# A linear-attention and expert kernel on one core: the Gram products at the end of an iteration, half of the spread transfers, a prologue in written-out order

## The chip, the cores and the metric

The kernel runs on one core of a Trainium2 chip. The metric is device time in microseconds (us) of one execution, as the median of several runs. Engines: PE is TensorE, DVE is VectorE, ACT is ScalarE, POOL is GpSimd, SP is SyncE, which here only issues DMAs. ACT issues DMAs too.

## The reference, cut to what matters

```python
k_n = k / (norm(k) + 1e-6)                     # (4, 8, 768, 48): 32 heads, 768 tokens, width 48
for t in range(S):                             # deltanet: one 48x48 state per head
    y[:, :, t] = q[:, :, t] @ state
    v_old = k_n[:, :, t] @ state
    state += beta[t] * outer(k_n[:, :, t], v[:, :, t] - v_old)
x = y.transpose(0, 2, 1, 3).reshape(3072, 384)
logits = x @ w_gate                            # 8 experts
expert = argmax(logits); gate_w = softmax(logits)[expert]
for e in range(8):                             # of each expert's tokens the 80 with the largest gate_w
    out[tok] = gate_w[tok] * (relu(x[tok] @ w1[e]) @ w2[e])
```

## The kernel before, in words

The 768 tokens of a head are cut into 12 chunks of 64, and a chunk of all 32 heads is worked on at once. Inside a chunk the recurrence becomes the inverse of a 64x64 triangular matrix per head. That inverse is built from 16x16 diagonal blocks: `solve` inverts them, and products with `XB` and `YB`, block-diagonal tiles that hold the small inverses, put the large inverse `Y` together.

What is done for chunk c, with the engine that does it:

- `load_k`, `load_q`, `load_v` fetch raw k (`kr`), q (`qn`) and v (`vin`); SP issues them.
- `squares` (ACT) and `newton` (DVE, some 15 small instructions) make 1/norm; `scale_k` (POOL) makes `kn`; `beta_mask` (POOL) makes a mask times beta.
- `trans`: PE transposes `kn` and `qn`, ACT copies the result to `KQ`.
- `gram`: PE multiplies `KQ` with itself; DVE turns each half into `B1` and `PT`; ACT issues two DMAs of `B1` to DRAM (`a_blocks`). `fetch` reads the 16x16 blocks back (`NT`); ACT issues it.
- `solve`: 30 POOL instructions on `NT` leave `XY`, the inverses and their transposes.
- `spread`: SP writes `XY` to DRAM (`inv_blocks`, named i_dram in the code) and then reads it back into `XB` with 8 small DMAs. `spread_t` reads it into `YB` with 4 DMAs of SP and 4 of ACT.
- `merge_p2` (needs `XB`), `merge_x4` (needs `YB`), `merge_y4`, `merge_p5`, `merge_y5`: PE products with an eviction each, on DVE (`P2`, half of `P5`) or ACT.
- The chain over the chunks: `chain_ks` (PE, then R on DVE), `chain_tr` (PE, then `UB` on DVE), `chain_qs`, `chain_ku` (updates the state in PSUM, ACT copies it to `SB`), `chain_pu` (ACT copies the output x, SP writes it to `x_rows`).
- `out_t` and `logits`: x is transposed, multiplied with the gate's weights, and DVE copies the result to `lg`. One part `zero` of the output is cleared per iteration by an SP DMA.

The order is written out by hand: each engine executes its instructions in the order of the program text. One loop over j from -4 to 11 is a software pipeline: iteration j does the chain of chunk j, the merges of j+1, the spread of j+2, `gram`, `fetch` and `solve` of j+3, and `scale_k` and `trans` of j+4. The first four iterations (j<0) are the prologue, with most calls empty.

Small DVE work that nobody waits for at once stands in a list of generators, `fillers`: `newton`; `gate` (some 24 instructions on the logits of a batch of three chunks); and `gate_top` (10 pairs of a maximum and a replacement, which keep the largest gate values). `fill(n)` puts the next n steps in at its place: 20 after `chain_pu`, 10 ahead of `merge_p2`, 4 after `logits`. Every third iteration `gate_pe` transposes gate values on PE, after `fill(100)` has emptied the list.

PSUM products share three buffers in rotation (`mtile`), so a product waits for the eviction of the third one before it. The DMAs of SP and ACT share eight completion semaphores in turn: a DMA also waits until the previous DMA on its semaphore has landed, whichever engine issued that one.

After the loop come the tail of the gate, the selection of 80 tokens per expert on DVE and PE, gathers on POOL, and the eight experts' products (`hp`, `yp`).

Of the kernel before, what the change touches and what calls it, by code (L numbers as in the profile page):

```python
# [24 lines left out]
def kernel(  # L25
# [22 lines left out]
    nc = tc.nc  # L48
# [105 lines left out]
    with ExitStack() as actx:  # L154
# [93 lines left out]
        def newton(bs):  # L248
# [4 lines left out]
            for n, c in enumerate(bs):  # L253
                nc.vector.tensor_reduce(ss[:, n * NB : (n + 1) * NB], ssq.pop(c), axis=AX, op=Alu.add)
                yield 1
            seed = sml.tile([128, 2 * NB], U32, name="seed")[:, :G]
            nc.vector.tensor_scalar(seed, ss.bitcast(U32), -0.5, 1597463007.0, op0=Alu.mult, op1=Alu.add)
            yield 1
            r = seed.bitcast(F32)
            for _ in range(3):  # L260
                t = sml.tile([128, 2 * NB], F32, name="nt")[:, :G]
                nc.vector.scalar_tensor_tensor(out=t, in0=ss, scalar=-0.5, in1=r, op0=Alu.mult, op1=Alu.mult)
                yield 1
                nc.vector.tensor_tensor(out=t, in0=t, in1=r, op=Alu.mult)
                yield 1
                rn = sml.tile([128, 2 * NB], F32, name="rn")[:, :G]
                nc.vector.scalar_tensor_tensor(out=rn, in0=t, scalar=1.5, in1=r, op0=Alu.add, op1=Alu.mult)
                yield 1
# [3 lines left out]
            yield 1  # L272
            nc.vector.tensor_scalar_add(n, n, 1e-6)
            yield 1
# [4 lines left out]
            yield 1  # L279

        def scale_k(c):
            if ok(c):
                nc.gpsimd.tensor_tensor(out=kn[c % NKB][:, :, 0:D], in0=kr.pop(c),
                                        in1=inv.pop(c).unsqueeze(2).to_broadcast([128, NB, D]), op=Alu.mult)
# [47 lines left out]
        def solve(c):  # L332
# [3 lines left out]
            XY = Xss[c] = sml.tile([128, 2, 16, 16], F32, name="XY")  # L336
            X = XY[:, 0]
            nc.gpsimd.tensor_tensor(out=X, in0=NT.rearrange("p s t -> p t s"), in1=eye16, op=Alu.add)  # L338
            for t in range(14, 0, -1):
                sh = [128, 15 - t, t]  # L340
                tmp = sml.tile([128, 64], F32, name="tmp")
                tv = tmp[:, : (15 - t) * t].rearrange("p (c s) -> p c s", s=t)
                nc.gpsimd.tensor_tensor(out=tv, in0=X[:, t + 1 :, t : t + 1].to_broadcast(sh),  # L343
                                        in1=NT[:, 0:t, t].unsqueeze(1).to_broadcast(sh), op=Alu.mult)
                nc.gpsimd.tensor_tensor(out=X[:, t + 1 :, 0:t], in0=X[:, t + 1 :, 0:t], in1=tv, op=Alu.add)  # L345
            nc.gpsimd.tensor_copy(XY[:, 1], X.rearrange("p t s -> p s t"))

        def spread(c):
# [4 lines left out]
            for e in range(2):  # L353
                for i in range(4):
# [3 lines left out]
        def spread_t(c, q):  # L358
# [156 lines left out]
        def gate(b):  # L515
# [4 lines left out]
            yield 1  # L520
            sh = sml.tile(full, F32, name="sh")
            nc.vector.tensor_tensor(out=sh, in0=l, in1=mx.unsqueeze(2).to_broadcast(full), op=Alu.subtract)
            yield 1
# [3 lines left out]
            yield 1  # L527
            fm = sml.tile([128, NT], F32, name="fm")
            nc.vector.tensor_reduce(fm, first, axis=AX, op=Alu.max)
            yield 1  # L530
            oh = sml.tile(full, F32, name="oh")
            nc.vector.tensor_tensor(out=oh, in0=first, in1=fm.unsqueeze(2).to_broadcast(full), op=Alu.is_equal)
            yield 1
            nc.vector.tensor_scalar_max(sh, sh, -87.0)
            yield 1
            n = sml.tile(full, F32, name="n")
            nc.vector.tensor_scalar(n, sh, LOG2E, None, op0=Alu.mult)
            yield 1
            nc.vector.tensor_scalar_add(n, n, ROUND)
            yield 1  # L540
            nc.vector.tensor_scalar_add(n, n, -ROUND)
            yield 1
            r = sml.tile(full, F32, name="r")
            nc.vector.scalar_tensor_tensor(out=r, in0=n, scalar=-LN2_HI, in1=sh, op0=Alu.mult, op1=Alu.add)
            yield 1
            nc.vector.scalar_tensor_tensor(out=r, in0=n, scalar=-LN2_LO, in1=r, op0=Alu.mult, op1=Alu.add)
            yield 1
            ex = sml.tile(full, F32, name="ex")
            nc.vector.tensor_scalar(ex, r, 1.0 / 5040.0, None, op0=Alu.mult)
            yield 1  # L550
            for f in (720.0, 120.0, 24.0, 6.0, 2.0, 1.0):
                nc.vector.scalar_tensor_tensor(out=ex, in0=ex, scalar=1.0 / f, in1=r, op0=Alu.add, op1=Alu.mult)
                yield 1
            nc.vector.tensor_scalar_add(ex, ex, 1.0)
            yield 1
            two = sml.tile(full, I32, name="two")
            nc.vector.tensor_scalar(two, n, 127.0, 8388608.0, op0=Alu.add, op1=Alu.mult)
            yield 1
            nc.vector.tensor_tensor(out=ex, in0=ex, in1=two.bitcast(F32), op=Alu.mult)
            yield 1  # L560
            gw = sml.tile([128, NT], F32, name="gw")
            nc.vector.tensor_reduce(gw, ex, axis=AX, op=Alu.add)
            yield 1
            nc.vector.tensor_scalar_add(gw, gw, 1e-9)
            yield 1
            nc.vector.reciprocal(gw, gw)
            yield 1
            og = ohg[:, b * NT : (b + 1) * NT, :]
            nc.vector.tensor_tensor(out=og, in0=oh, in1=gw.unsqueeze(2).to_broadcast(full), op=Alu.mult)
            yield 1  # L570
# [22 lines left out]
        def gate_top(b):  # L593
            cd, nx = cand[b % 2], cand[(b + 1) % 2]
            for t in range(TR):
                m8 = nx[:, t * 8 : t * 8 + 8]
                nc.vector.max(m8, cd)
                nc.vector.match_replace(cd, in_to_replace=m8, in_values=cd, imm_value=0.0)
                yield 1
# [6 lines left out]
        load_k(0)  # L606
# [15 lines left out]
        for c in squares([0]):  # L622
            for _ in newton([0]):
                pass
        nc.vector.tensor_copy(beta_t.rearrange("r c g -> r (c g)"), bps[:, 0, : NB * NC])
        S_ps = ps_s.tile([128, 2, 512], F32, name="S_ps")
        nc.vector.memset(S_ps, 0.0)
        nc.vector.memset(zero, 0.0)
        nc.vector.tensor_copy(P5.rearrange("r p g w -> r (p g) w"), eye.unsqueeze(1).to_broadcast([128, NB, 64]))

        for j in range(-4, NC):
            spread(j + 2)
            chain_ks(j)
# [18 lines left out]
            fill(20)  # L652
# [15 lines left out]
            if j >= GC and j % GC == 0:  # L668
# [3 lines left out]
            if j >= 0 and j % GC == GC - 1:  # L672
                fill(100)
# [168 lines left out]
```

## Time and the profile before

| | us |
|---|---|
| median of 3 runs | 514.31 (513.81 to 514.63) |
| the profiled execution, its own time | 510.11 |
| its span, first to last instruction | 508.1 |
| PE busy, all of the span | 354.1 |
| POOL busy | 190.6 |
| DVE busy | 213.2 |
| ACT busy | 117.5 |

`UB` is written once per chunk, by `chain_tr`; its first DVE instruction marks the iterations. In the profiled execution it starts at 89.88, 114.08, 139.97, 168.24, 193.79, 220.38, 244.22, 272.57, 293.39, 315.65, 336.47 and 351.88 us for the chunks 0 to 11. So the prologue lasts 89.88 us, the eleven intervals 262.0 us and what follows 156.2 us.

### The profile page before, as it was taken

The page shows a single profiled execution, that of the slowest core. Times are in us where ns is not written, and L with a number is a line of the kernel's source. Part 1 is how long each engine was busy: PE and PEld are TensorE (multiplying, and loading weights), DVE is VectorE, ACT ScalarE, POOL GpSimd, SP SyncE. Part 2 cuts the span into 40 slices and gives each one's busy share as a digit, 9 for nine tenths or more (in the row PEclk, how much of TensorE's full clock was granted, in tenths as well). Part 3 has the DMA queues.
Part 4 walks back from the last instruction along what each step waited for, and adds up shares of the span by engine and source line. Part 5 has one row for each costly group of instructions (what it writes and reads, how often), then busy time and mean ns, then how long its engine had stood idle before and what let it go on. Part 6 is the DMA issues. An engine that isn't in the chain of part 4 may idle for free. (4 is left out here: it accounts for less than half of the span.)

```text
span 508.1 us, 16641 instructions
## 1 busy us (share of the span) xinstructions
PE 354.1 (70%) x7227; PEld 311.8 (61%) x7239; DVE 213.2 (42%) x545; ACT 117.5 (23%) x207; POOL 190.6 (38%) x476
## 2 busy tenths in 40 slices
PE   2632574969695979697958996876100269999996
PEld 2632463959595968596847886876100167777773
DVE  4823202632353555833474923637659600010100
ACT  2120141606151434133321450422100000010000
POOL 8727576636272563618380725100200140000010
PEclk9965687979788899889979998989655557999999
DMA  9362857484819293746473454412739965980000
GB/s 163 66 113 66 121 108 149 75 178 84 176 30 204 37 186 70 165 83 131 95 157 65 107 100 114 83 38 65 234 107 409 411 220 161 316 294 15 10 17 14
DMA packets 198728, 66.48 MB, mean 131 GB/s; under 512 B 180704, under 2 KB 191968, under 8 KB 198656
## 3 DMA queue, kind: packets, MB, share of 16 engines
q1 hardware_dynamic: 134656, 54.69, 42.2%
q10 hardware_dynamic: 63232, 8.77, 10.5%
q0 software_dynamic: 768, 1.97, 1.3%
q8 instruction: 57, 0.93, 0.8%
q14 instruction: 15, 0.12, 0.1%
HBM read 45.53 MB, written 19.86 MB: 129 GB/s over the span
## 5 line engine op out<-in xcount | busy, mean ns | idle before, releaser
L343 POOL TENSOR_TENSOR tmp<-XY,NT 128x14 f32<-128x14 f32 (+6 forms) x168 | 48.2, 287 | 13.2
L338 POOL TENSOR_TENSOR XY<-NT,eye 128x256 f32<-128x256 f32 x12 | 10.2, 851 | 110.0 <-DMA NT<-a_blocks 110.0
L345 POOL TENSOR_TENSOR XY<-XY,tmp 128x14 f32<-128x14 f32 (+6 forms) x168 | 45.8, 273 | 13.2
L802 PEld LDWEIGHTS hp<-xTe,w 128*128 128x128 f32 x384 | 49.0, 210 | 2.1 <-issue 1.2
L207 PE MATMUL pm<-P,YB 64*64 64x32 f32 x768 | 22.7, 279 | 37.7 <-DMA YB<-inv_blocks 35.8
L802 PE MATMUL hp<-xTe,w 128*128 128x80 f32 x384 | 48.8, 292 | 0.0
L453 DVE TENSOR_TENSOR UB<-pm,beta_t 64x768 f32<-64x768 f32 x24 | 22.9, 955 | 60.2 <-PE pm L207 59.9
L207 PEld LDWEIGHTS pm<-P,YB 64*64 64x64 f32 x768 | 21.8, 206 | 39.5 <-issue 39.5
L810 PE MATMUL yp<-w,hT 128*80 128x384 f32 x128 | 44.0, 498 | 0.0
L814 POOL DMA_INDIRECT out_dram<-y,idx_s x8 | 7.4, 923 | 83.8 <-DVE y L813 83.8
L207 PE MATMUL pm<-KQ 48*64 48x128 f32 x768 | 29.2, 311 | 12.7 <-ACT KQ L301 7.1
L805 ACT ACTIVATE hT<-hp 128x320 f32<-128x320 f32 x16 | 7.0, 437 | 133.7 <-PE hp L802 133.7
L380 DVE TENSOR_TENSOR P<-pm,mask 128x512 f32<-128x512 f32 x24 | 15.5, 686 | 49.4 <-PE pm L207 49.4
L207 PE MATMUL pm<-SB,KQ 128*64 128x96 f32 x704 | 35.0, 254 | 1.2 <-DVE lg L511 1.2
L390 ACT COPY X<-pm 128x512 f32<-128x512 f32 x12 | 7.0, 586 | 122.4 <-PE pm L207 72.6
L207 PEld LDWEIGHTS pm<-KQ 48*64 48x64 f32 x768 | 25.8, 157 | 14.8 <-ACT KQ L301 7.8
L301 ACT COPY KQ<-pm 128x512 f32<-128x512 f32 x48 | 24.9, 613 | 34.8 <-PE pm L298 24.3
L207 PEld LDWEIGHTS pm<-SB,KQ 128*64 128x64 f32 x704 | 31.2, 141 | 2.2 <-PE pm L590 1.5
L810 PEld LDWEIGHTS yp<-w,hT 128*80 128x80 f32 x128 | 19.1, 155 | 20.2 <-issue 20.2
L207 PE MATMUL pm<-XB,B 128*64 128x128 f32 x384 | 25.3, 288 | 6.2 <-DMA YB<-inv_blocks 3.9
L207 PEld LDWEIGHTS pm<-XB,B 128*64 128x64 f32 x384 | 22.3, 144 | 9.6 <-issue 5.2
L813 DVE TENSOR_SCALAR y<-yp,gw_t 80x384 f32<-80x384 f32 x8 | 4.9, 613 | 54.7 <-PE yp L810 54.7
(163 smaller groups left out, 663.8 us busy)
## 6 DMA issues: line engine op xcount, KB each, us to landing
w<-in_moe_w_dram SPq DMA_DIRECT2D x16, 1536.0 KB, 7.3
a_blocks<-B ACTq DMA_DIRECT2D x24, 256.0 KB, 4.6
vin<-in_v_dram SPq DMA_DIRECT2D x26, 192.0 KB, 4.8
kr<-in_k_dram SPq DMA_DIRECT2D x24, 192.0 KB, 3.9
qn<-in_q_dram SPq DMA_DIRECT2D x24, 192.0 KB, 4.6
x_rows<-x SPq DMA_DIRECT2D x24, 192.0 KB, 2.7
out_dram<-zero SPq DMA_DIRECT2D x12, 384.0 KB, 2.6
inv_blocks<-XY SPq DMA_DIRECT2D x12, 256.0 KB, 2.9
```

Of the source, the lines that this page charges most:

```text
L207: nc.tensor.matmul(out, lhsT=lhsT, rhs=rhs, start=not acc, stop=not acc, skip_group_check=True)
L301: nc.scalar.copy(KQs[c][:, 4 * h : 4 * h + 4, n, :], pt[:, h].rearrange("r (g w) -> r g w", w=128))
L338: nc.gpsimd.tensor_tensor(out=X, in0=NT.rearrange("p s t -> p t s"), in1=eye16, op=Alu.add)
L343: nc.gpsimd.tensor_tensor(out=tv, in0=X[:, t + 1 :, t : t + 1].to_broadcast(sh), in1=NT[:, 0:t, t].unsqueeze(1).to_broadcast(sh), op=Alu.mult)
L345: nc.gpsimd.tensor_tensor(out=X[:, t + 1 :, 0:t], in0=X[:, t + 1 :, 0:t], in1=tv, op=Alu.add)
L380: nc.vector.tensor_tensor(out=P2[:, p].rearrange("r g e w -> r (g e) w"), in0=ps[:, p].rearrange("r (g w) -> r g w", w=64), in1=mask.unsqu ...
L390: nc.scalar.copy(X4s[c], ps[:, :, :256].rearrange("r b (g w) -> r b g w", w=32))
L453: nc.vector.tensor_tensor(out=UB[hs(e), :, e].rearrange("r (g c) d -> r c g d", c=2), in0=ps[hs(e), :, : 8 * D].rearrange("r c (g d) -> r ...
L802: nc.tensor.matmul(hp[:, (f - f0) * cap : (f - f0 + 1) * cap], lhsT=w1_t[:, c, f * 128 : (f + 1) * 128], rhs=xTs[e][:, c, :], start=(c == ...
L805: nc.scalar.activation(hT[:, f0:f1, :], hp[:, : (f1 - f0) * cap].rearrange("p (f t) -> p f t", t=cap), Act.Relu)
L810: nc.tensor.matmul(yp[:cap, :DM], lhsT=hT[:, f, :], rhs=w2_t[:, f, :], start=(f == 0), stop=(f == FK - 1))
L814: nc.gpsimd.indirect_dma_start(out=out[:, :], out_offset=bass.IndirectOffsetOnAxis(ap=idx_s[:, e : e + 1], axis=0), in_=y[:, :], element_o ...
```

## The change

`gram(j+4)` stands at the end of iteration j, between `out_t` and `logits`, where `gram(j+3)` stood near the start. `fetch(j+3)` and `solve(j+3)` follow `merge_p5`; `scale_k` and `beta_mask` of j+4 stand at the top; `merge_p2(j+2)` stands ahead of `out_t`. `spread` issues only the blocks that the later product with `mask` keeps (4 DMAs into `XB`, not 8). `spread_t` issues all 8 into `YB` on SP, right after `merge_y4`, and so ahead of the loads. `fill` takes an estimate in us (0.5 and 7.0 in an iteration), and each filler step names its own estimate. `gate_pe` moves one iteration later (j = 4, 7, 10). The prologue is written out; `solve(0)` and `solve(1)` run on DVE there.

```diff
-        def fill(n):
-            while n > 0 and fillers:
-                if next(fillers[0], None) is None:
+        def fill(us):
+            while us > 0 and fillers:
+                n = next(fillers[0], None)
+                if n is None:
                     fillers.pop(0)
                 else:
-                    n -= 1
+                    us -= n
...
-        def solve(c):
+        def solve(c, eng=nc.gpsimd):
...
             for e in range(2):
-                for i in range(4):
+                for i in (0, 2):
                     r = 64 * e + 16 * i
                     nc.sync.dma_start(XB[r : r + 16, :, e, 16 * i : 16 * i + 16], src[e, i, 0])
...
-            for h in range(2):
-                for i in range(4):
+            for i in range(4):
+                for h in range(2):
                     r = 64 * h + 16 * i
-                    if h == q:
-                        eng = (nc.sync, nc.scalar)[q]
-                        eng.dma_start(YB[r : r + 16, :, h, 16 * i : 16 * i + 16], src[h, i, 1])
+                    eng = nc.scalar if c == 0 and h else nc.sync
+                    eng.dma_start(YB[r : r + 16, :, h, 16 * i : 16 * i + 16], src[h, i, 1])
...
+        warm = sml.tile([128, 1], F32, name="warm", bufs=1)
+        nc.scalar.activation(warm, ident[:, 0:1], Act.Square)
...
+        trans(2, 1, qn[2 % NQB])
+        load_q(3)
+        fetch(0)
+        gram(2)
+        for t in (XB, YB, SB, UB):
+            nc.gpsimd.memset(t, 0.0)
+        solve(0, nc.vector)
+        spread(0)
+        spread_t(0)
+        fetch(1)
+        norms([3])
+        scale_k(3)
+        beta_mask(3)
+        load_k(6)
+        trans(3, 0, kn[3])
+        trans(3, 1, qn[3 % NQB])
+        load_q(4)
+        solve(1, nc.vector)
+        fetch(2)
+        solve(2)
+        nc.vector.memset(zero, 0.0)
+        nc.vector.tensor_copy(P5.rearrange("r p g w -> r (p g) w"), eye.unsqueeze(1).to_broadcast([128, NB, 64]))
+        merge_p2(0)
+        spread(1)
+        merge_x4(0)
+        norms([4])
+        merge_y4(0)
+        merge_p5(0)
+        spread_t(1)
+        gram(3)
+        merge_y5(0)
+        merge_p2(1)
+
-        for j in range(-4, NC):
+        for j in range(NC):
+            if j % GC == GC - 1 and j > GC:
+                gate_pool(j // GC - 1)
+            scale_k(j + 4)
+            beta_mask(j + 4)
             spread(j + 2)
             chain_ks(j)
             if j % 2 == 0:
-                bs = squares([j + 5, j + 6])
-                fillers.insert(0, newton(bs))
-            gram(j + 3)
+                fillers.insert(0, newton(squares([j + 5, j + 6])))
             merge_x4(j + 1)
+            chain_tr(j)
+            merge_y4(j + 1)
+            spread_t(j + 2)
+            fill(0.5)
+            merge_p5(j + 1)
             fetch(j + 3)
-            chain_tr(j)
-            fill(40 if j == -3 else 0)
-            merge_y4(j + 1)
-            merge_p5(j + 1)
+            solve(j + 3)
             chain_qs(j)
             chain_ku(j)
-            scale_k(j + 4)
-            beta_mask(j + 4)
-            if j % GC == 1 and j > GC:
-                gate_pool(j // GC - 1)
-            solve(j + 3)
             chain_pu(j)
-            fill(20)
             load_k(j + 7)
             load_q(j + 5)
             load_v(j + 2)
-            spread_t(j + 2, 0)
-            if 0 <= j < zr.shape[0]:
+            if j < zr.shape[0]:
                 nc.sync.dma_start(zr[j], zero)
+            fill(7.0)
             merge_y5(j + 1)
             trans(j + 4, 0, kn[(j + 4) % NKB])
             trans(j + 4, 1, qn[(j + 4) % NQB])
+            merge_p2(j + 2)
             out_t(j)
-            spread_t(j + 2, 1)
-            fill(10)
-            merge_p2(j + 2)
+            gram(j + 4)
             logits(j)
-            fill(4)
-            if j >= GC and j % GC == 0:
+            if j > GC and j % GC == 1:
                 fill(100)
                 gate_pe(j // GC - 1)
                 fillers.append(gate_top(j // GC - 1))
-            if j >= 0 and j % GC == GC - 1:
-                fill(100)
+            if j % GC == GC - 1:
                 fillers.append(gate(j // GC))
```

How SP's queue stands in one iteration of the loop (j=3, from the write of the inverses on), before:

```order
L351 DMA inv_blocks<-XY 128x512
L356 DMA XB<-inv_blocks 16x16x16 x8
L491 DMA x_rows<-x 64x2x384 x2
L226 DMA kr<-in_k_dram 64x16x48 x2
L232 DMA qn_163<-in_q_dram 64x16x48 x2
L239 DMA vin<-in_v_dram 64x16x48 x2
L367 DMA YB<-inv_blocks 16x16x16 x4
L658 DMA out_dram<-zero 128x768
```

The same stretch of SP's queue in the changed kernel:

```order
L353 DMA inv_blocks<-XY 128x512
L358 DMA XB<-inv_blocks 16x16x16 x4
L368 DMA YB<-inv_blocks 16x16x16 x8
L492 DMA x_rows<-x 64x2x384 x2
L228 DMA kr<-in_k_dram 64x16x48 x2
L234 DMA qn_163<-in_q_dram 64x16x48 x2
L241 DMA vin<-in_v_dram 64x16x48 x2
L710 DMA out_dram<-zero 128x768
```

All of `YB` now stands ahead of the seven other issues, and SP has four DMAs of `YB` more and four of `XB` fewer.

On PE, from the transposes of `kn` to `chain_tr` of the next chunk, before (`B`, `P` and `SB` are B1, P2 and the state):

```order
L298 MATMUL pm<-ident,kn_157 128x128 x8
L298 MATMUL pm<-ident,qn_163 128x128 x8
L499 MATMUL pm<-ident,x 128x128 x6
L373 LDWEIGHTS identb
L373 MATMUL pm<-eyes,identb 128x512
L373 LDWEIGHTS identb
L373 MATMUL pm<-eyes,identb 128x512
L207 MATMUL pm<-XB,B_926 64x128 x16
L509 MATMUL pm<-wg,xT 64x8 x12
L207 MATMUL pm<-SB,KQ 64x96 x16
L207 MATMUL pm<-KQ 64x128 x32
L207 MATMUL pm<-P_1735,YB 64x32 x32
```

The same stretch of PE in the changed kernel:

```order
L300 MATMUL pm<-ident,kn_157 128x128 x8
L300 MATMUL pm<-ident,qn_163 128x128 x8
L374 LDWEIGHTS identb
L374 MATMUL pm<-eyes,identb 128x512
L374 LDWEIGHTS identb
L374 MATMUL pm<-eyes,identb 128x512
L207 MATMUL pm<-XB,B_869 64x128 x16
L500 MATMUL pm<-ident,x 128x128 x6
L207 MATMUL pm<-KQ 64x128 x32
L510 MATMUL pm<-wg,xT 64x8 x12
L207 MATMUL pm<-SB,KQ 64x96 x16
L207 MATMUL pm<-P_1732,YB 64x32 x32
```

The Gram product (`pm<-KQ`) moved from behind the state product (`SB,KQ`) to ahead of the logits (`wg,xT`), and the product with `XB` moved ahead of the transposes of x.

## Rows read from the trace of the kernel before

**Rows 1.** Windows cut at starts of UB: length, busy (PE, PEld, DVE, ACT, POOL), clock, DMA share

```profile
0.00:89.88 89.88, 42.81 (x788) 39.00 (x792) 33.07 (x76) 19.04 (x31) 58.25 (x141) 0.77 0.63 112
...
114.08:293.39 179.31, 145.19 (x3917) 136.45 (x3925) 96.34 (x241) 62.22 (x109) 89.56 (x236) 0.90 0.58 114
272.57:293.39 20.82, 18.59 (x561) 17.51 (x562) 15.37 (x43) 8.16 (x15) 9.23 (x30) 1.00 0.51 107
293.39:315.65 22.26, 17.02 (x481) 15.74 (x484) 4.99 (x8) 6.95 (x12) 9.16 (x30) 0.92 0.54 112
315.65:336.47 20.82, 16.64 (x482) 15.56 (x485) 10.13 (x35) 6.40 (x11) 2.31 (x7) 0.92 0.36 73
336.47:351.88 15.41, 12.29 (x384) 11.29 (x386) 11.70 (x37) 5.81 (x10) 0.00 (x0) 1.00 0.19 55
```

**Rows 2.** Waits of PE within the eleven intervals: us in total, times, longest

```profile
PE pm L207 <- DMA YB<-inv_blocks: 28.5, 7, 5.6
```

**Rows 3.** Timeline of PE, two stretches: start, us, instructions, idle before and releaser

```profile
213.53 3.69 PE L207 MATMUL pm<-KQ 48*64 48x128 f32 x64 [4.88 <-DVE lg L511]
...
264.86 0.38 PE L590 MATMUL pm<-ident,ohg 128*48 128x128 f32 x1 [5.79 <-DVE ohg L569]
```

**Rows 4.** Timeline of SP's issues in one iteration

```profile
194.07 4.92 SPq L356 DMA_DIRECT2D XB<-inv_blocks  x8
201.75 1.25 SPq L491 DMA_DIRECT2D x_rows<-x  x2
203.10 1.40 SPq L226 DMA_DIRECT2D kr<-in_k_dram  x2
204.54 4.01 SPq L232 DMA_DIRECT2D qn<-in_q_dram  x2
208.67 1.86 SPq L239 DMA_DIRECT2D vin<-in_v_dram  x2
210.64 2.85 SPq L367 DMA_DIRECT2D YB<-inv_blocks  x4
```

**Rows 5.** Waits of SP's queue within the eleven intervals

```profile
SPq L351 <- DMA a_blocks<-B: 16.7, 5, 8.6
```

**Rows 6.** DMA issues: count, KB each, median us from issue to landing

```profile
a_blocks<-B ACTq DMA_DIRECT2D x24, 256.0 KB, 4.6
...
inv_blocks<-XY SPq DMA_DIRECT2D x12, 256.0 KB, 2.9
NT<-a_blocks ACTq DMA_DIRECT2D x12, 128.0 KB, 3.6
XB<-inv_blocks SPq DMA_DIRECT2D x96, 16.0 KB, 3.1
```

**Rows 7.** Timelines of the prologue: kr's norms, the solves on POOL, the last wait

```profile
5.73 1.28 ACT L245 ACT_TABLE_LOAD   x1 [5.73 <-DMA kr<-in_k_dram]
...
34.02 0.85 POOL L338 TENSOR_TENSOR XY<-NT,eye 128x256 f32<-128x256 f32 x1 [8.46 <-DMA NT<-a_blocks]
...
45.60 1.47 POOL L283 TENSOR_TENSOR kn<-kr,inv 128x768 f32<-128x768 f32 x1
...
66.08 1.48 POOL L283 TENSOR_TENSOR kn<-kr,inv 128x768 f32<-128x768 f32 x1
...
86.16 1.93 PE L207 MATMUL pm<-P,YB 64*64 64x32 f32 x64 [7.29 <-DMA YB<-inv_blocks]
```

**Rows 8.** Timeline of DVE: a small instruction beside POOL's solve, one with POOL idle

```profile
202.06 0.33 DVE L264 TENSOR_TENSOR nt<-nt,rn 128x32 f32<-128x32 f32 x1
...
359.21 0.21 DVE L522 TENSOR_TENSOR sh<-lg,mx 128x48 f32<-128x48 f32 x1
```

**Rows 9.** Timeline of DVE: first of ten gate_top pairs and what follows them; the last lg

```profile
279.41 0.37 DVE L597 MAX8 cand<-cand 48x8 f32<-48x208 f32 x1
...
288.06 1.29 DVE L380 TENSOR_TENSOR P<-pm,mask 128x512 f32<-128x512 f32 x2
...
358.77 0.17 DVE L511 COPY lg<-pm 128x16 f32<-128x16 f32 x1 [4.97 <-PE pm L509]
```

More of the change, by code (lines that the diff above doesn't have):

```diff
@@ L278, in newton, with scale_k @@
                 inv[c] = iv[:, n * NB : (n + 1) * NB]
-            yield 1
-        def scale_k(c):
+            yield 0.2
+        def scale_k(c, eng=nc.gpsimd):
             if ok(c):
-                nc.gpsimd.tensor_tensor(out=kn[c % NKB][:, :, 0:D], in0=kr.pop(c),
+                eng.tensor_tensor(out=kn[c % NKB][:, :, 0:D], in0=kr.pop(c),
                                         in1=inv.pop(c).unsqueeze(2).to_broadcast([128, NB, D]), op=Alu.mult)
@@ L335, in solve @@
             NT = NTs.pop(c)
-            XY = Xss[c] = sml.tile([128, 2, 16, 16], F32, name="XY")
+            XY = Xss[c] = sml.tile([128, 2, 16, 16], F32, name="XY", bufs=3)
             X = XY[:, 0]
-            nc.gpsimd.tensor_tensor(out=X, in0=NT.rearrange("p s t -> p t s"), in1=eye16, op=Alu.add)
+            eng.tensor_tensor(out=X, in0=NT.rearrange("p s t -> p t s"), in1=eye16, op=Alu.add)
             for t in range(14, 0, -1):
                 sh = [128, 15 - t, t]
-                tmp = sml.tile([128, 64], F32, name="tmp")
+                tmp = sml.tile([128, 64], F32, name=f"tmp{eng is nc.gpsimd}")
                 tv = tmp[:, : (15 - t) * t].rearrange("p (c s) -> p c s", s=t)
-                nc.gpsimd.tensor_tensor(out=tv, in0=X[:, t + 1 :, t : t + 1].to_broadcast(sh),
+                eng.tensor_tensor(out=tv, in0=X[:, t + 1 :, t : t + 1].to_broadcast(sh),
                                         in1=NT[:, 0:t, t].unsqueeze(1).to_broadcast(sh), op=Alu.mult)
-                nc.gpsimd.tensor_tensor(out=X[:, t + 1 :, 0:t], in0=X[:, t + 1 :, 0:t], in1=tv, op=Alu.add)
-            nc.gpsimd.tensor_copy(XY[:, 1], X.rearrange("p t s -> p s t"))
+                eng.tensor_tensor(out=X[:, t + 1 :, 0:t], in0=X[:, t + 1 :, 0:t], in1=tv, op=Alu.add)
+            eng.tensor_copy(XY[:, 1], X.rearrange("p t s -> p s t"))
         def spread(c):
@@ L612 @@
         load_q(0)
+        load_q(1)
         load_v(0)
+        load_v(1)
+        warm = sml.tile([128, 1], F32, name="warm", bufs=1)
+        nc.scalar.activation(warm, ident[:, 0:1], Act.Square)
         for t in kn + qn:
             nc.vector.memset(t[:, :, D:], 0.0)
-        for t in (XB, YB, SB, UB):
-            nc.gpsimd.memset(t, 0.0)
+        S_ps = ps_s.tile([128, 2, 512], F32, name="S_ps")
+        nc.vector.memset(S_ps, 0.0)
         bps = mtile()
@@ L621, with norms @@
                 mm(bps[hs(e), 0, NB * c : NB * c + NB], braw[:, C * c : C * c + C], sel_h[:, e].rearrange("r p g c -> r (p g c)"))
-        for c in squares([0]):
-            for _ in newton([0]):
-                pass
+        def norms(bs):
+            for _ in newton(squares(bs)):
+                pass
+        norms([0])
+        scale_k(0, nc.vector)
         nc.vector.tensor_copy(beta_t.rearrange("r c g -> r (c g)"), bps[:, 0, : NB * NC])
-        S_ps = ps_s.tile([128, 2, 512], F32, name="S_ps")
-        nc.vector.memset(S_ps, 0.0)
+        beta_mask(0)
+        load_k(3)
+        trans(0, 0, kn[0])
+        trans(0, 1, qn[0])
+        norms([1, 2])
+        gram(0)
+        scale_k(1)
+        beta_mask(1)
+        load_k(4)
+        trans(1, 0, kn[1])
+        trans(1, 1, qn[1])
+        load_q(2)
+        gram(1)
+        scale_k(2)
+        beta_mask(2)
+        load_k(5)
+        trans(2, 0, kn[2])
+        trans(2, 1, qn[2 % NQB])
[18 more added lines that the diff above has]
+        solve(2)
         nc.vector.memset(zero, 0.0)
         nc.vector.tensor_copy(P5.rearrange("r p g w -> r (p g) w"), eye.unsqueeze(1).to_broadcast([128, NB, 64]))
-        for j in range(-4, NC):
+        merge_p2(0)
[13 more added lines that the diff above has]
+            beta_mask(j + 4)
             spread(j + 2)
```

65 lines of the change are left out of this document (33 added, 32 removed).

## The prediction

> **What bounds the kernel now.** I read the page of the profile first, then the execution cut into windows at the starts of `UB`, then the waits inside the loop, and last the timelines of the places that the waits name.
>
> The windows show three parts [rows 1]. The prologue takes 89.88 us with PE busy for 42.81. The eleven intervals take 262.0 us, and the seven full ones among them, 114.08 to 293.39, take 179.31 us, 25.6 each. What follows the last `UB` takes 156.2 us, and the diff leaves it alone but for one filler. The reader should compare the mean of 25.6 with the fastest full interval, 272.57 to 293.39: 20.82 us, PE busy for 18.59, and the only row of the seven at a granted clock of 1.00 [rows 1]. The same number of products is done in each of them, so what the other six lose is waiting and clock, not work. In all seven PE is busy for 145.19 us; at 18.59 each that would be 130.1. So 15.1 us of PE's time are the same products run at a lower clock.
>
> The waits say what for. PE waits 28.5 us for `YB` in the loop [rows 2], at `merge_x4`. It waits 4.88 us behind `lg` at 213.53 and 5.79 us for the gate at 264.86 [rows 3]. The first of these two is DVE's order: `gram` could not start because `lg` and `P2` stood behind fillers. Ten pairs of `gate_top` take from 279.41 to 288.06, 0.865 us a pair, and `P2` starts the moment they end [rows 9]. So the loop is held neither by PE's work nor by POOL's, but by when `YB` lands and by what stands ahead of `P2` and `lg` on DVE.
>
> Why `YB` is late is seen on SP [rows 4]: after the `XB` issues (194.07) come `x_rows`, `kr`, `qn`, `vin`, and only at 210.64 `YB`, 11.65 us after the last `XB` was issued.
>
> **The change, part by part.** *`YB` ahead of the loads, half of `XB`.* One `XB` issue costs 4.92/8 = 0.62 us and one `YB` issue 2.85/4 = 0.71 [rows 4]. Four fewer `XB` and four more `YB` on SP are +0.4 us of SP's time, and ACT loses its four. `YB` comes 11.65 us earlier, more than any single wait. The chain from `gram` to `YB`: two issues of `a_blocks` (an estimate of 1.2 at 0.62 each) and 4.6 to land, `NT` 0.6 and 3.6, the solve 11.6 (34.02 to 45.60), `inv_blocks` 0.6 and 2.9, four `XB` 2.5, eight `YB` 5.7, and 3.1 to land: 36.4 us [rows 4, 6, 7]. From the end of `gram(j+3)`, now the end of iteration j-1, to `merge_x4(j+3)` are two iterations and some 3 us of logits and `chain_ks`: 43.4 us at 20.2 each. The slack is 7.0 us, so I take the whole 28.5 as gone. The loads pay: they stand some 8 us later. `vin` and `qn` are used an iteration or more after they are loaded, and this covers it; if the cover were gone, the price would be that delay.
>
> *`gram` at the end, `merge_p2` ahead of `out_t`.* Same products, other order. `gram` now covers ACT's copy of `xT` ahead of the logits. `chain_ks` loses the cover that `gram` gave R on DVE; `merge_x4` alone stands between. I cost this at 0.4 us an iteration, an estimate.
>
> *Doses.* 7 us of fillers stand after `chain_pu`, where DVE waits for `merge_p2` behind several PE steps, so `P2`, `B1` and `lg` no longer stand behind ten pairs. The waits of 4.88 and 5.79 go.
>
> *Iteration time.* PE alone needs at least 18.59 [rows 1]. SP needs, per iteration, 2.46 (`XB`), 5.70 (`YB`), 1.25, 1.40, 4.01 and 1.86 for the other pairs [rows 4], 2.9 for the landing of `inv_blocks` before `XB` [rows 6], and two single issues at 0.62 for `inv_blocks` and `zero`: 20.8. With `qn` at `vin`'s 1.86 it is 18.6. The two bounds are close, and the best interval of before, 20.82, is the upper end. I take 20.2, nearer the upper end because two queues that are nearly full will meet.
>
> Intervals 1 to 7: 7 x 20.2 = 141.4, against 179.3. Interval 0 has no `chain_ks` and no `chain_qs`: 18, against 24.2. The last three have no transposes or `gram` of later chunks. They were 22.26, 20.82 and 15.41 with PE busy 17.02, 16.64 and 12.29 at clocks of 0.92, 0.92 and 1.00 [rows 1]; I take 17.3, 17 and 14.3. The eleven sum to 208.0 instead of 262.0, a gain of 54.0. A second way gives the same: 28.5 + 4.88 + 5.79 of waits and 15.1 of clock are 54.3.
>
> *Prologue.* The table load of 1.28 us leaves `kr`'s path [rows 7]. `solve(0)` waits for `NT` until 34.02 before [rows 7]; now `NT(0)` stands behind the copies of `KQ(2)` on ACT and the solve behind `gram(2)` on DVE. No row shows a solve on DVE. Its 28 small instructions take from 0.21 (POOL idle) to 0.33 (beside POOL's solve) [rows 8], so 5.9 to 9.2 us and some 1.5 for its first and last, against 11.6 on POOL. I take 8.5. I put the end of `solve(0)` at 47.5, 1.9 later than before, since norms, three `gram`s and memsets crowd ahead. `NT(1)` follows four `YB` issues on ACT that wait for `inv_blocks`, about 8 us, and lands 3.6 later: 59. `solve(1)` ends at about 67 (66.08 before [rows 7]). Then `P2(0)`, `merge_x4(0)`, `merge_y4(0)` (8 us by an estimate), eight `YB` that land 8.8 after that, and `merge_x4(1)` and `chain_tr(0)`, 2.7: `UB(0)` at 86.5. I take 86, with 80 and 96 as ends. Before, the last step waited 7.29 us for `YB` [rows 7].
>
> The solves on DVE bring the case for a rule. The row shows 0.33 beside POOL and 0.21 alone, 0.12 more an instruction [rows 8], or 3.4 us a solve, which is within my 8.5. The Trainium skill, "SBUF — State Buffer", section "Who interferes with whom", says that a DVE instruction with two SBUF inputs and a GpSimd instruction that reads SBUF lock each other out for the whole instruction. By it each small instruction of `solve(1)` would wait for a POOL instruction while POOL works.
>
> *Tail.* `gate_top(2)` starts one iteration later and runs in j=11. Its ten pairs and `UB`'s 1.9 end 10.6 us after `UB(11)` starts, where `lg` was ready 6.9 after it (358.77 against 351.88) [rows 9]: +3.7.
>
> *Sum.* 86.0 + 208.0 = 294.0 for `UB(11)`, against 351.88: -57.9. With the tail, -54.2. The profiled execution's own time of 510.11 would become 455.9. The median of the runs is 4.2 higher, and I take the same difference from it: 514.3 - 54.2 = 460.1.
>
> **The rivals.** *A. SP becomes the bound.* The DMAs of SP and ACT share eight semaphores, and SP waited 16.7 us in five places for `a_blocks` at the write of `inv_blocks` [rows 5], 3.3 each. In the changed kernel `a_blocks` waits for a `YB` landing and the next `XB` or `zero` for `a_blocks`. If that adds its 3.3 to an SP sum of 18.6 to 20.8, an iteration takes 21.9 to 24.1; at 22.7 the time is 7 x 2.5 = 17.5 us higher, 478. For it speaks how full SP is; against it that `a_blocks` is issued at the end of an iteration, by my estimate some 10 us after `YB`, so most of these landings are past.
>
> *B. The prologue loses.* Each of `solve(1)`'s 28 instructions waits for one of POOL's, 0.25 us: an estimate between the two durations of [rows 8]: 28 x 0.25 = 7 us, and `UB(0)` comes at 93: 467. This is the rule cited above. Against it: POOL has little to do between `beta_mask(3)` and `solve(2)`.
>
> *C. `YB` stays late.* The slack of 7.0 is used up by SP standing behind `zero` and by POOL doing `scale_k`, `beta_mask` first. If half of the 28.5 stays, the time is 474.
>
> *D. Slower than before.* The wait for `a_blocks` at SP goes to its longest, 8.6 [rows 5], in every iteration, because `a_blocks` now leaves at the end of an iteration, just ahead of the next `inv_blocks`. On 20.8 that is 29.4 an iteration, 64 us more than forecast: 524. It decides from 27.9 on, where 7 x 7.7 eats the 54.2: a wait of 7.1 every time. Against it: before, only five waits of this kind were there, and their mean was 3.3.
>
> **Chances.** Forecast 0.58 (by itself 446 to 470: an iteration of 18.9 to 21.2 is -9 to +7, the prologue's ends -6 to +10), A 0.20, B 0.09, C 0.06, D 0.07. The range reaches from 446 to A's time and a little over, 481; above it lie D and the worse part of A, and below it little. A measurement of this kernel tells some 0.2% from no change. Faster 0.92, within 0.2% 0.01, slower 0.07.
>
> **What would show it.** Right: intervals of about 20 with a clock near 1.00, no wait of PE for `YB` in the loop, `UB(0)` near 86, `lg` held by `gate_top` in the tail. Wrong: SP's queue waiting for `a_blocks` or `YB` in each iteration (A, D), POOL or DVE instructions in `solve(1)` of twice the length (B), PE still waiting for `YB` (C). The forecast fails most easily where two full queues, PE and SP, wait for each other in turn.

## The result and the profile after

The changed kernel takes 476.05 us (median of 4 runs, 473.19 to 478.13) against 514.06 of the kernel before (510.58 to 514.63): a ratio of 0.927, 95% interval 0.920 to 0.934. The forecast was 460 with a range of 446 to 481. The profiled execution took 473.19 us, its span 471.5. A ratio leaves out runs that lie more than 1.5% above the fastest of the same kernel in its set, so it need not equal the ratio of the medians.

The windows of the changed kernel, cut at starts of `UB` (length, busy time of PE, PEld, DVE, ACT, POOL, granted clock, DMA share, GB/s); they answer to [rows 1]:

```profile
0.00:86.76 86.76, 40.79 (x790) 36.51 (x792) 50.08 (x150) 19.14 (x32) 38.54 (x80) 0.76 0.61 108
86.76:105.78 19.02, 18.42 (x530) 16.55 (x531) 12.74 (x28) 8.51 (x15) 9.66 (x31) 1.00 0.70 131
105.78:261.00 155.22, 141.03 (x3924) 128.11 (x3926) 86.77 (x211) 63.15 (x110) 91.07 (x238) 0.98 0.67 137
129.62:149.27 19.65, 19.42 (x562) 17.80 (x564) 12.56 (x27) 8.50 (x15) 9.94 (x31) 1.00 0.54 114
215.89:239.78 23.89, 21.37 (x562) 19.30 (x564) 16.77 (x48) 8.45 (x15) 14.32 (x33) 0.93 0.71 156
261.00:279.27 18.27, 16.32 (x482) 14.40 (x484) 12.98 (x38) 6.50 (x11) 9.22 (x31) 1.00 0.46 87
279.27:296.96 17.69, 15.81 (x482) 14.22 (x484) 10.04 (x33) 6.49 (x11) 2.31 (x7) 1.00 0.43 96
296.96:311.83 14.87, 12.85 (x385) 11.60 (x387) 4.09 (x8) 5.81 (x10) 0.00 (x0) 1.00 0.20 58
311.83:471.50 159.67, 100.72 (x658) 75.64 (x658) 52.51 (x154) 8.65 (x19) 18.54 (x30) 0.78 0.50 176
```

`UB(0)` comes at 86.76 (forecast 86). What follows `UB(11)` takes 159.67 (forecast 156.2 + 3.7). The eleven intervals take 225.07, and were forecast at 208.0. So the whole miss lies in the loop, and 13.8 us of it in the seven full intervals: 22.2 us each instead of 20.2. The best of them, 129.62 to 149.27, takes 19.65; the first, third and sixth of the seven took 23.8 to 25.2.

The waits of PE in the seven intervals (total us, times, longest); they answer to [rows 2, 3]:

```profile
PE pm L207 <- issue: 11.3, 8, 3.0
PE pm L207 <- DVE lg L512: 1.7, 2, 0.9
PE pm L207 <- DVE UB L454: 1.1, 5, 0.2
```

No wait for `YB` is left, nor for the gate. In their place stands "issue", a wait for which the profile has no releaser: 11.3 us, where the kernel before had 5.0 in its seven. The timeline of PE shows what such a wait looks like:

```profile
169.76 1.36 PE L207 MATMUL pm<-R,Y 64*64 64x48 f32 x63
174.17 0.25 PE L207 MATMUL pm<-R,Y 64*64 64x48 f32 x1 [3.04 <-issue]
```

63 of the 64 products of `chain_tr` ran, and the last one came 3.04 us later. All 64 read the same tiles, so no buffer or semaphore of the program lies between them. What lies there is seen in the DMA queues. The stretch 165.6 to 171.8 of the changed kernel, and then 171.8 to 172.9 (queue: packets, MB, share of 16 engines):

```profile
q1 hardware_dynamic: 3311, 0.83, 67.7%
q10 hardware_dynamic: 1075, 0.27, 19.4%
```

```profile
q10 hardware_dynamic: 867, 0.22, 88.4%
q1 hardware_dynamic: 387, 0.07, 32.9%
q8 instruction: 1, 0.02, 5.3%
```

For 6.2 us the queue of instructions (q8) moved nothing while `x_rows`, `kr`, `qn`, `vin` and `a_blocks` filled the engines; then one packet came, and PE went on 1.4 us after it. In the trace each of the eight "issue" waits of the seven intervals ends 1.3 to 1.7 us after the end of such a packet. The packets ahead of seven of them start 5.6 to 7.8 us after the one before, the one ahead of the shortest (0.34 us) 3.8. Of the packets without a wait behind them most come 3.3 to 5.1 us after the one before, but four come 6.1 to 6.7 after it, so a late packet doesn't always stop PE. The Trainium skill, "Runtime: NRT & Kernel Launch", section "Instruction fetch mechanics", says that the sequencer refills its instruction buffer by DMA in blocks of 256 instructions, and that the cost is mostly hidden. The trace agrees on the block (PE's 14,478 instructions and 57 packets of 0.93 MB are 254 a packet), and on the hiding in part: 8 of the 32 packets of the seven intervals have such a wait behind them.

### The profile page after: what moved, and what is told of

It is laid out like the page before. It is cut to its first block, busy times and chain, and to the rows that moved or that the text cites. A ratio compares the mean times of both kernels' runs of the same rounds, so it can differ in the third digit from the quotient of the medians.

```text
span 471.5 us, 16602 instructions
## 1 busy us (share of the span) xinstructions
PE 345.9 (73%) x7239; PEld 297.0 (63%) x7239; DVE 229.2 (49%) x619; ACT 118.3 (25%) x208; POOL 169.3 (36%) x415
## 5 line engine op out<-in xcount | busy, mean ns | idle before, releaser
L345 POOL TENSOR_TENSOR tmpTrue<-XY,NT 128x14 f32<-128x14 f32 (+6 forms) x140 | 39.9, 285 | 11.0
L347 POOL TENSOR_TENSOR XY<-XY,tmpTrue 128x14 f32<-128x14 f32 (+6 forms) x140 | 38.4, 274 | 11.0
L300 PE MATMUL pm<-ident,kn 128*128 128x128 f32 x96 | 16.2, 323 | 29.5 <-POOL kn L285 27.7
L340 POOL TENSOR_TENSOR XY<-NT,eye 128x256 f32<-128x256 f32 x10 | 8.6, 856 | 71.1 <-DMA NT<-a_blocks 71.1
L300 PEld LDWEIGHTS pm<-ident,kn 128*128 128x128 f32 x96 | 12.8, 166 | 31.0 <-POOL kn L285 28.2
L207 PE MATMUL pm<-YB,P 128*64 128x128 f32 x384 | 26.0, 289 | 2.6 <-issue 2.6
L207 PE MATMUL pm<-KQ 48*64 48x128 f32 x768 | 25.6, 285 | 2.9 <-ACT KQ L303 2.9
L285 POOL TENSOR_TENSOR kn<-kr,inv 128x768 f32<-128x768 f32 x11 | 16.4, 1490 | 31.4 <-DVE inv L278 31.4
L207 PEld LDWEIGHTS pm<-KQ 48*64 48x64 f32 x768 | 22.4, 140 | 5.5 <-ACT KQ L303 4.0
L207 PEld LDWEIGHTS pm<-YB,P 128*64 128x64 f32 x384 | 22.5, 144 | 3.7 <-issue 3.1
```

The source lines that it names most:

```text
L207: nc.tensor.matmul(out, lhsT=lhsT, rhs=rhs, start=not acc, stop=not acc, skip_group_check=True)
L285: eng.tensor_tensor(out=kn[c % NKB][:, :, 0:D], in0=kr.pop(c), in1=inv.pop(c).unsqueeze(2).to_broadcast([128, NB, D]), op=Alu.mult)
L300: nc.tensor.transpose(pt[:, g // 4, (g % 4) * 128 : (g % 4) * 128 + 128], src[:, 2 * g : 2 * g + 2, :].rearrange("r p d -> r (p d)"), ident)
L340: eng.tensor_tensor(out=X, in0=NT.rearrange("p s t -> p t s"), in1=eye16, op=Alu.add)
L345: eng.tensor_tensor(out=tv, in0=X[:, t + 1 :, t : t + 1].to_broadcast(sh), in1=NT[:, 0:t, t].unsqueeze(1).to_broadcast(sh), op=Alu.mult)
L347: eng.tensor_tensor(out=X[:, t + 1 :, 0:t], in0=X[:, t + 1 :, 0:t], in1=tv, op=Alu.add)
```

## The experiments

Times of the kernel before differ between the four sets of runs (medians 514.1, 515.9, 509.0 and 512.5), so kernels of different sets are compared by their ratio to the kernel before, and within a set by their times. "Seven" is the time from `UB(1)` to `UB(8)` in the profiled execution. Theory F says that PE's instruction packets come late when the DMA engines are full. Theory P is that PE eats instructions faster than they can come, whatever the traffic. Theory S is that SP's full queue sets the interval.

**1. No loads in the loop** (one run).

```diff
+        krf, vinf = kr[6], vin[1]
         for j in range(NC):
...
-            load_k(j + 7)
-            load_q(j + 5)
-            load_v(j + 2)
+            if ok(j + 7):
+                kr[j + 7] = krf
+            if ok(j + 2):
+                vin[j + 2] = vinf
```

> The changed kernel without the loads of kr, qn and vin inside the loop (kr of chunk 6, vin of chunk 1 and the q of the prologue stand in, so the later chunks are computed from other data). Seven full intervals between UB(1) and UB(8) took 155.2 us in the changed kernel, 11.3 us of them PE idle with no visible releaser (issue). Theory F, late instruction packets because the DMA engines are full with loads and a_blocks: issue waits fall below 4 us, the seven intervals to 142 or less. Rival P, PE simply eats its instructions faster than they can come: issue waits stay between 9 and 13 us, the intervals above 150. Rival S, SP's full queue sets the interval: the intervals fall, but the issue waits do not go in step with them.

474.58 us; seven 151.71. The waits of PE in them:

```profile
PE pm L207 <- issue: 4.0, 4, 2.0
PE pm L300 <- ACT x L489: 3.4, 2, 2.4
PE pm L207 <- DVE lg L512: 1.7, 2, 0.9
```

The issue waits fell to 4.0, which P excludes. The seven intervals fell by 3.5 only and not to F's 142: two new waits, 3.4 us together, appeared for x, behind ACT, and PE was still busy for 140.3. The eleven intervals together didn't fall at all, 225.83 against 225.07:

```profile
86.60:312.43 225.83, 206.03 (x5785) 186.71 (x5796) 126.21 (x315) 90.13 (x157) 111.91 (x305) 0.97 0.39 85
```

The last three took 18.75, 21.69 and 14.90 where the changed kernel took 18.27, 17.69 and 14.87, the first two of them at clocks of 0.91 and 0.92, the second with a wait of 3.1 us for `XB`. So most of the issue waits go with the loads, but this run doesn't show that the loads cost the loop any time. SP's queue lost six of its issues of an iteration and the loop was as long, so S falls too.

**2. More traffic, not on SP** (one run).

```diff
                 nc.scalar.dma_start(ad[e, :, : 64 * 64].rearrange("g (r w) -> r g w", w=64), B1[hs(e)])
+            if c >= 4:
+                for e in range(2):
+                    nc.scalar.dma_start(idle[hs(e)], kf.rearrange("(g e) (c t) d -> e c t g d", e=2, t=C)[e, c, :, :12])
...
+        idle = blk.tile([128, 12, D], F32, name="idle")
```

> The changed kernel with 144 KB more to load per iteration, issued by ACT right behind a_blocks into a tile that nothing reads; SP's queue is unchanged. Theory F: issue waits of PE in the seven intervals rise from 11.3 to 16 or more and the time by 4 to 10 us. Rival P: issue waits stay at 9 to 13 us, the time within 2 us. Rival S: the time moves only as far as SP's issues take longer, with the issue waits unchanged.

The two DMAs of an iteration move 144 KB each, so the dose was 288 KB, twice what the expectation says. 477.41 us; seven 159.51, 4.3 more. Issue waits 11.1, and 1.3 more of the same kind at the state product: 12.4, not 16. Another 1.6 us are waits for `X` on ACT, which issued the new DMAs. F had the sign of the intervals but not the size of the waits; this run doesn't support it.

**3. `YB` behind the loads.**

```diff
             merge_y4(j + 1)
-            spread_t(j + 2)
             fill(0.5)
...
             load_v(j + 2)
+            spread_t(j + 2)
```

> The changed kernel with the eight YB issues behind kr, qn and vin instead of ahead of them. By the prediction's step YB lands some 8 us later than the changed kernel's, more than the slack: PE waits for YB return, 2 to 4 us an interval, and the time goes to 490 or above. Rival: the new order of gram and solve alone has made the room, and the time stays within 3 us.

518.99 us, ratio 1.019 (1.007 to 1.031): no faster than the kernel before, with everything else of the change in place. Seven 185.15. The first wait of PE in them:

```profile
PE pm L207 <- DMA YB<-inv_blocks: 33.1, 7, 7.2
```

One wait in each interval, and no issue wait at all in the seven, with the loads in place. The eleven intervals take 271.76 us, 46.7 more than in the changed kernel. With `YB` behind the loads the rest of the change gains nothing. (All eight `YB` issues stand there in this run. In the kernel before it was four of them, and ACT issued the others, so the 46.7 can overstate what the place is worth.)

**4. `YB` ahead of the loads, in the kernel before.**

```diff
-                        eng = (nc.sync, nc.scalar)[q]
+                        eng = nc.sync
...
             merge_y4(j + 1)
+            spread_t(j + 2, 0)
+            spread_t(j + 2, 1)
...
-            spread_t(j + 2, 0)
...
-            spread_t(j + 2, 1)
```

> The kernel before with one part of the change: all eight YB issues on SP right after merge_y4, ahead of the loads. By the prediction's step the 28.5 us of waits for YB in the loop go, and with them 15 to 28 us of the time: 487 to 499. Rival: the wait only moves (solve is as late as before, or the loads come late), and the time falls by less than 8 us.

489.89 us, ratio 0.964 (0.950 to 0.979): about half of the change's gain by the ratios. In the profiled execution `UB(0)` comes at 80.93, 9.0 us earlier, and the eleven intervals take 248.6, 13.4 less. Its waits of PE in the seven intervals (171.87):

```profile
PE pm L207 <- issue: 7.3, 7, 2.1
PE pm L207 <- DVE lg L511: 6.7, 3, 4.6
PE pm L590 <- DVE ohg L569: 4.1, 1, 4.1
PE pm L207 <- DMA YB<-inv_blocks: 3.9, 2, 2.6
PE S_ps L207 <- issue: 3.1, 2, 1.8
```

The wait for `YB` is nearly gone, 12.0 less than the 15.9 of the kernel before in its seven; the waits for `lg` and for the gate are still there, and 10.4 of issue waits, 7.3 and 3.1, stand where 5.0 stood. In the changed kernel the two waits for DVE are nearly gone; that the doses and the gate's place do this is read from the waits, and no run changes these alone.

**5. The solves of the prologue on POOL.**

```diff
-        solve(0, nc.vector)
+        solve(0)
...
-        solve(1, nc.vector)
+        solve(1)
```

> The changed kernel with solve(0) and solve(1) back on POOL. If the solves on DVE are a gain of the prologue: 11.7 us each instead of the 7.9 and 11.3 of the changed kernel, and POOL reaches solve(2) later, so UB(0) comes 4 to 9 us later than 86.8 and the time is 4 to 10 us higher. Rival: the lock-out between DVE and POOL, which stretched two instructions of solve(1) to 1.8 and 1.3 us, takes away what DVE gains, and UB(0) stays within 2 us of 86.8.

477.32 us; `UB(0)` at 90.28, 3.5 later than in the changed kernel and 5.0 later than in its repeat (run 9), seven 155.77. The solves on DVE are worth some 3.5 to 5 us at `UB(0)`.

**6. `gram` at the start of an iteration.**

```diff
-        gram(3)
...
+            gram(j + 3)
             merge_x4(j + 1)
...
             out_t(j)
-            gram(j + 4)
             logits(j)
```

> The changed kernel with gram(j+3) back after chain_ks at the start of iteration j, all else as changed. If gram's place carries the slack of YB: a_blocks leaves some 3 us later, B1 and PT stand ahead of UB on DVE, and the eleven intervals (225 us) grow by 5 to 20 us. Rival: YB's place alone carries it, and the eleven intervals stay within 4 us of 225.

Times of 472.58 to 484.13, median 481.69, with no ratio: too wide to tell. The profiled execution (472.58) has eleven intervals of 225.86 against 225.07. PE's waits for the logits' input are new, one in each interval:

```profile
PE pm L510 <- ACT xT L502: 6.6, 7, 0.9
```

That is the cover that the prediction spoke of, 0.94 us an iteration. It is paid for elsewhere: PE's busy time in the seven fell from 141.03 to 137.11, at a clock of 1.00 instead of 0.98. `gram`'s place carries no slack that counts in this profile.

**7. The clearing DMAs in the last four iterations.**

```diff
-            if j < zr.shape[0]:
-                nc.sync.dma_start(zr[j], zero)
+            if j >= NC - 4:
+                for z in range(3 * (j - NC + 4), 3 * (j - NC + 4) + 3):
+                    nc.sync.dma_start(zr[z], zero)
```

> The changed kernel with the twelve clearing DMAs of 384 KB taken out of the busy iterations: three in each of the last four. Theory F (late instruction packets from full DMA engines): issue waits of PE in the seven intervals fall from 11.3 to about 8, the seven intervals by 4 to 8 us, and the time by 3 to 7 us. Rival P (PE's own pace): issue waits and the time stay, within 2 us. Rival S (SP's full queue): the intervals fall by SP's 0.5 to 2 us each, issue waits unchanged.

473.97 us, ratio 0.935 (0.928 to 0.941); seven 154.70, issue waits 10.1. This can't be told from no change.

**8. Norms of chunk 3 ahead of the solve.** In the changed kernel DVE stood still between its two solves, from 48.4 to 54.2 us, because of this row of ACT:

```profile
53.29 0.84 ACT L247 ACTIVATE sq<-kr 128x768 f32<-128x768 f32 x1 [17.18 <-DMA XB<-inv_blocks]
```

The squares need only `kr(3)`, but in ACT's order they stand behind four `YB` issues that wait for `inv_blocks`, and so does `NT(1)`.

```diff
+        norms([3])
         fetch(0)
         gram(2)
+        fetch(1)
         for t in (XB, YB, SB, UB):
             nc.gpsimd.memset(t, 0.0)
+        scale_k(3)
+        beta_mask(3)
         solve(0, nc.vector)
         spread(0)
         spread_t(0)
-        fetch(1)
-        norms([3])
-        scale_k(3)
-        beta_mask(3)
```

> The changed kernel with norms(3) ahead of gram(2), and fetch(1), scale_k(3) and beta_mask(3) ahead of solve(0). In the changed kernel DVE waited from 48.4 to 54.2 for the squares of chunk 3, which stood on ACT behind YB's issues. If that order is what holds the prologue: solve(1) starts as solve(0) ends, UB(0) comes at 73 to 78 instead of 86.8, and the time falls by 8 to 13 us. Rival: NT(1) or XB(0) is late instead and UB(0) stays above 82.

469.09 us, ratio 0.924 (0.917 to 0.931), which isn't told from the changed kernel's 0.927; `UB(0)` at 81.60. The second solve did start as the first ended, at 49.86, but `UB(0)` gained 5.2 us (3.7 against the repeat in run 9) and not 9 to 14. SP's waits from 40 to 90 us name what was late next:

```profile
SPq L368 <- DMA a_blocks<-B: 5.4, 1, 5.4
```

One `YB` issue stood for 5.4 us for the landing of `a_blocks(3)`, on whose completion semaphore it came next.

**9. The changed kernel again**, as a measure for the next three, which ran on the same chip with it.

> The changed kernel once more, to stand on the same chip as the three below. All theories: 470 to 478, UB(0) at 86 to 88, the seven intervals 153 to 158, PE issue waits in them 9 to 12.

474.58 us (472.81 to 477.89), ratio 0.938 (0.931 to 0.945); seven 155.99, issue waits 9.7, `UB(0)` at 85.33. Runs 5, 8 and 10 leave the seven intervals as they are, so five profiles show how far equal ones differ: 155.2 to 156.0 in length and 9.6 to 11.3 in issue waits. Their eleven intervals, which differ a little at the ends, take 223.9 to 226.3. Smaller differences mean nothing.

**10. Prologue and tail together:** the edit of 8, and

```diff
         spread_t(1)
-        gram(3)
         merge_y5(0)
         merge_p2(1)
+        gram(3)
...
-            if j > GC and j % GC == 1:
+            if (j > GC and j % GC == 1 and j < 10) or j == 9:
```

> The changed kernel with norms(3), fetch(1), scale_k(3) and beta_mask(3) early (as in the run before), gram(3) of the prologue behind merge_p2(1), and the last gate_pe one iteration earlier (after j=9). In the run before one YB issue waited 5.4 us for the landing of a_blocks(3), and x4(1) 5.1 us for YB; gram(3) later takes that away: UB(0) at 75 to 78. The gate's move gives back the 3.5 us of the tail: 156 to 157 from UB(11) to the end. Together 14 to 16 us under the changed kernel on the same chip. Rival: solve(2) becomes what is late, the second interval grows, and the gain stays under 9 us.

464.15 us (461.33 to 468.78), ratio 0.914 (0.905 to 0.923): 10.4 us under the changed kernel, where 14 to 16 were expected. `UB(0)` came at 80.81, not 75 to 78: `YB`'s wait is gone, but `solve(0)` ended 3.6 us later than in the changed kernel. The tail, `UB(11)` to the end:

```profile
307.11:463.40 156.29, 101.23 (x658) 75.84 (x658) 44.57 (x124) 8.66 (x19) 18.61 (x30) 0.79 0.51 179
```

Against 160.55 in the changed kernel beside it, the tail's 4 us are back. Runs 11 and 12 have the same prologue, and there `UB(0)` came at 79.26 and 78.17, so a difference of 2 us at `UB(0)` means little.

**11. `kr` ahead of `YB`**, on top of 10.

```diff
             merge_y4(j + 1)
+            load_k(j + 7)
             spread_t(j + 2)
...
-            load_k(j + 7)
             load_q(j + 5)
```

> The kernel above with the two kr loads of an iteration ahead of YB instead of behind x_rows, into a stretch where the DMA engines are nearly idle. Theory F (late instruction packets): issue waits in the seven intervals fall from about 10 to 7 or less, the intervals by 3 to 6 us. Rival: YB, 1.4 us later, meets the end of its slack, waits for YB come back and the intervals do not fall. Theory P: neither moves.

463.96 us, ratio 0.918 (0.909 to 0.928); seven 153.69 and issue waits 8.2, where 10 had 155.94 and 11.2, and no wait for `YB`. The waits and the seven intervals moved the way of F, the intervals by less than it said; the eleven took 225.45, within the spread of run 9, and the time did not move.

**12. The clearing DMAs late**, on top of 10, with the edit of 7.

> The kernel c5 with the twelve clearing DMAs in the last four iterations. Theory F: issue waits 1 us lower, as in the earlier run of this part alone (11.3 to 10.1), the intervals 0 to 3 us lower. Theory P: no change in either.

463.05 us (458.55 to 464.51), ratio 0.914 (0.908 to 0.920); seven 152.48, issue waits 9.2. The seven intervals lie 2.7 us below the spread of run 9, and the eleven, 223.02, 0.9 below it. The median is 11.5 us under the changed kernel on its chip and within the spread of run 10.

## Why the prediction was right, and where it was not

**The sum.** The measured time lies in the stated range, but above the 446 to 470 that the forecast had by itself: only because the range was drawn out to rival A's time does it hold the 476, and A's mechanism isn't what happened. That the range held is luck, though the parts of the mechanism below are not. The prediction also took a measurement to tell 0.2% from no change; the medians of the kernel before in the four sets, 509.0 to 515.9, differ by 1.4%.

**`YB` and the loads.** Right that the wait goes: the 28.5 us of [rows 2] are gone, they are nearly gone where only this part was put in (run 4), and with `YB` behind the loads the wait is back (run 3). Too high was the value of the part by itself: in run 4 the eleven intervals fell by 13.4 us, because other waits came out from under it. The price of the loads that now stand behind it did not show as a wait of PE.

**The gate and the doses.** Right in the loop: of 4.88 and 5.79 us [rows 3] 1.7 is left, at `lg`. The doses, the gate's place, the place of `merge_p2` and the four `XB` DMAs left out were not run by themselves, so what each is worth isn't shown.

**The iteration.** Here the term was mis-sized: 20.2 us became 22.2. The first step that went wrong is the floor. It was read as 18.59, PE's busy time in one interval [rows 1], and all that PE was busy beyond seven times that, 15.1 us, was put down to the clock. The granted clock did rise, from 0.90 to 0.98, but PE's busy time in the seven fell from 145.19 to 141.03, by 4.2 us. An interval in which PE hardly ever stops takes 19.65 with the new order and is busy for 19.42, and in run 6, at a clock of 1.00 throughout, the seven were still busy for 137.11, 19.6 each. Why that one interval before had only 18.59 stays open. The second is the issue wait, which the sum had at nothing: 11.3 us, where the kernel before had 5.0. The missing 10.9 of clock and the 6.3 of waits take 17.2 us off the 54.3 of the prediction's second way and leave 37.1; the eleven intervals fell by 36.9. So the two ways agreed only because both had the same errors.

As a budget: with 19.65 as the floor the seven intervals would take 137.6. The 11.3 of issue, the 1.7 of `lg` and 5.1 us by which PE's busy time exceeds seven times 19.42, part of it in intervals at a clock of 0.93, add up to 155.7, against 155.2 measured. That the kernel before hid part of the issue waits, since PE's instructions had time to come while it stopped for `YB`, is argued and not tested by itself; run 3 fits it, with 33.1 us of such stops and no issue wait in the seven.

**Rival A** came out with nearly the measured time, 478, by a mechanism that isn't what PE waits for. The longest of SP's waits for `a_blocks` in the changed kernel, over its whole span:

```profile
SPq L710 <- DMA a_blocks<-B: 4.5, 1, 4.5
SPq L358 <- DMA a_blocks<-B: 4.4, 1, 4.4
SPq L353 <- DMA a_blocks<-B: 3.2, 1, 3.2
```

Two of them lie in the eleven intervals (four, of 13.5 us together, in the repeat of run 9), not one per iteration, and PE waits for neither `XB` nor `YB`. Run 1 took six issues of an iteration from SP, and the loop was as long. Rival D falls with A.

**What causes the issue waits** is settled in part. That PE stops for instructions is read from the order of events, packet by packet; no run shows it in another way. That the traffic makes the packets late rests on run 1 (11.3 to 4.0) and on where the late packets lie. Runs 2, 7, 11 and 12 changed the traffic by less and gave 12.4, 10.1, 8.2 and 9.2, within or near the 9.6 to 11.3 of equal kernels. Run 1 didn't shorten the eleven intervals, so what the loop would gain if the packets came in time isn't shown, and how much each kind of transfer delays a packet stays open.

**The prologue** was right in sum (86.76 against 86), in part because errors cancel: `solve(0)` ended at 48.4 (47.5 was said) and `solve(1)` at 69.1 (67), and from there to `UB(0)` it took 17.7 us where the terms add up to 19.5. The sum hides something else. The kernel before with nothing but `YB` moved has `UB(0)` at 80.93 (run 4), 4 to 6 us ahead of the changed kernel with its written-out prologue. The order of ACT's work that run 8 puts right is worth about that.

Rival B's mechanism is there, but in three instructions. DVE in `solve(0)`, then in `solve(1)`:

```profile
41.13 0.18 DVE L345 TENSOR_TENSOR tmpFalse<-XY,NT 128x14 f32<-128x14 f32 x1
...
58.36 1.29 DVE L345 TENSOR_TENSOR tmpFalse<-XY,NT 128x14 f32<-128x14 f32 x1
59.68 1.81 DVE L347 TENSOR_TENSOR XY<-XY,tmpFalse 128x14 f32<-128x14 f32 x1
...
67.40 0.85 DVE L347 TENSOR_TENSOR XY<-XY,tmpFalse 128x26 f32<-128x26 f32 x1
```

And POOL at that time:

```profile
57.99 1.62 POOL L285 TENSOR_TENSOR kn<-kr,inv 128x768 f32<-128x768 f32 x1 [23.05 <-DVE inv L278]
59.57 1.90 POOL L291 TENSOR_TENSOR bm<-beta_t,neg_strict 128x1024 f32<-128x1024 f32 x1
67.36 0.84 POOL L340 TENSOR_TENSOR XY<-NT,eye 128x256 f32<-128x256 f32 x1 [5.89 <-DMA NT<-a_blocks]
```

Each of the three DVE instructions ends within 0.05 us of a POOL instruction: 1.29, 1.81 and 0.85 us instead of 0.18, 0.17 and 0.19 in `solve(0)`. The Trainium skill, "SBUF — State Buffer", section "Who interferes with whom", says that a DVE instruction with two inputs from SBUF contends with a POOL instruction that reads SBUF. The trace agrees. The cost was 3.4 us, all that `solve(1)` (11.3 us) took longer than `solve(0)` (7.9), and not the 7 us of rival B: POOL ran two long instructions beside `solve(1)` and began `solve(2)` only at its end, so not 28 of them waited.

**The tail** was right: `lg(11)` waited for the last `gate_top` pair.

```profile
322.08 0.35 DVE L600 MATCH_REPLACE8 cand<-cand,cand 48x208 f32<-48x208 f32 x1
322.46 0.17 DVE L512 COPY lg<-pm 128x16 f32<-128x16 f32 x1
```

That is 10.6 us after `UB(11)` (311.83), as said, and run 10 gave the loss back.

## What to carry to other kernels

Where one queue issues most of the DMAs, look at their order before their number: moving `YB` ahead was worth 13.4 us of the old loop, while six issues fewer left the new loop as long as it was. Put first what the next stage waits for, and loads that are used an iteration later behind it. A wait that is taken away uncovers the next one, so a floor read from busy time should be taken from a stretch that has no waits, and forecasts near it should leave room. An engine's in-order queue also holds what doesn't wait: squares that needed only `kr` stood behind issues that waited for something else, and moving them, with what follows them, gave 4 to 5 us at `UB(0)`.

## What the runs showed of the hardware that was not expected

PE stopped in the middle of a product for up to 3.0 us, 11.3 us in seven iterations of some 1,126 PE instructions each, and each time went on 1.3 to 1.7 us after the end of a packet of the instruction queue. Where PE waited for data in every iteration (run 3), no such stop was left. One DVE instruction of 0.18 us took 1.81 us beside a POOL instruction of 1.90.
